# First feed-forward layer: the positive part is written over its PSUM bank, with a new set of planning numbers

## The chip, the cores and the metric

One NeuronCore of a Trainium2 chip runs the whole program. The metric is the time of one execution on the device in microseconds (us). Engines have these names: PE is TensorE (PEld is its weight load), DVE is VectorE, ACT is ScalarE, POOL is GpSimd, SP is the queue that issues the DMAs.

## What is computed

Attention with a hashed mask, then a feed-forward layer with softplus (the layer of the change), then a gated one with SiLU. Shapes: 2 batches, 8 heads, 768 positions, 64 per head; 1536 tokens of 512 for the two layers.

```python
mask = q_bucket[:, :, :, None] == k_bucket[:, :, None, :]
scores = np.where(mask, scale * q @ k.T, -1e9)
attn = exp(scores - max) / (sum + 1e-9)
x = (attn @ v)                       # 1536 x 512
h = x @ w_in                         # 512 -> 2048
g = np.maximum(h, 0.0) + np.log1p(np.exp(-np.abs(h)))
x = g @ w_out                        # 2048 -> 512
gate = x @ w_gate; val = x @ w_val   # 512 -> 1536
out = (gate / (1 + np.exp(-gate)) * val) @ w_out2
```

## The kernel before, in words

Values are split into a high and a low 16-bit part, and a product is three matmuls (L1134 to L1136). The tokens are four chunks of 384, two of each batch. The program has three stages that overlap. Batch 0's attention (scores in fp32, L869, row maximum L888) comes first, while DVE, ACT and POOL unpack the weights of FFN 1. Batch 1's attention (L876, L893) follows, and the matmuls of FFN 1 for chunks 0 and 1 are strewn into it. Then chunks 2 and 3 of FFN 1 run densely on PE while the gate weights are unpacked (L408, L413, L419, L446, L452, L458, L462), and from there FFN 2 (L1262 to L1307) keeps PE to the end.

A tile of FFN 1 is 128 of the 2048 inner features by the 384 tokens of a chunk: 16 tiles a chunk, 64 in all. Its steps, in `ffn1`: 12 matmuls into a PSUM bank `f` (for batch 1, every second tile takes a bank of the ring `z` instead); `mag` on ACT (L1158, |h| into the SBUF tile `fa`); `relu` on DVE (L1163, the positive part into the SBUF tile `fr`); `ex` and `ln` on ACT (L1174, L1177, in place in `fa`); `add` on DVE (L1180, `fr` = `fa` times a scale + `fr`); the high part `g` by ACT, POOL or DVE (L1185, L1188, L1191), the low part on POOL (L1194). Before the change the bank is free once `mag` and `relu` have read it. The ring `f` has two banks, taken in turn; the planes (products with the hash projection, L602 and L607, whose signs DVE takes at L618, or ACT at L627 with POOL at L632), the sums over partitions (L359) and the turned queries (L799) use the same two. Of `fr` and `fa` there are two each.

Nobody writes the order by hand. The class `Order` takes all steps with a length, an engine (or several ways, with a penalty `BV` each) and an urgency (due time plus an offset `U`), and lists them greedily: the step that can start first, but among those of the same engine that could start within `SLACK` of it, the most urgent. Each engine then runs its list strictly in that order. So a different `SLACK`, `BV` or `U` changes the order on every engine and which engine does a step; it doesn't change what is computed.

Of the kernel before, what the change touches and what calls it, by code (L numbers as in the profile page):

```python
# [55 lines left out]
class Order:  # L56
# [5 lines left out]

    LAT = {"EE": 0.0, "AA": 0.15, "GG": 0.1, "VV": 0.13, "EA": 0.2, "EV": 0.2}
    DMA = 1.25, 0.95
    SLACK = 0.1067
    PORT = 0.75

    def __init__(self, rings):
# [120 lines left out]
def tile_hash_attention__softplus_ffn__silu_glu(  # L189
# [39 lines left out]
    def stt(n):  # L229
        return 0.13 + n / 960.0  # L230
# [10 lines left out]
    def pe(cols):  # L241
        return 0.04 + cols / 2400.0

    BV = dict(ck=0.865, re=1.809, st=-2.309, tf=0.612, th=1.227, hi=2.138, lo=5.114, slo=0.082, wlo=0.046, bits=-0.999, meas=1.623, cv=-0.593, ca=0.592)
    U = dict(st=0, vl=0, tp=-20.24, th=-2, tl=-1.85, w2=51.64, qp=-7.63, kp=-4.93, kv=3.56, f1=0.25, y=40, ev=-5.28, ex=2.63, hi=-7.89, lo=2.67, gw=422.36, x=3.11)

    const = ctx.enter_context(tc.tile_pool(name="const", bufs=1))
    xyp = ctx.enter_context(tc.tile_pool(name="xyp", bufs=1))
# [34 lines left out]
    def ways(urgency, opts, after=(), takes=(), uses=(), line=None):  # L283
        return order.step(urgency, opts, after, takes, uses, line)
# [21 lines left out]
    def new(pool, shape, dt, slot):  # L306
        slot.t = pool.tile(shape, dt, tag=slot.ring, name=nm(slot.ring), bufs=RINGS[slot.ring])
        return slot.t
# [829 lines left out]
    def ffn1(c, due, x_ready, w1_ready, g_ready, w2_ready, y_ready):  # L1138

        b = chunks[c][0]  # L1140
        gs, g_done, hs = [], [], []
        for m in range(K1):
            f, fa, fr, g = (Slot(x) for x in ("z" if b == B - 1 and m % 2 else "f", "fa", "fr", "g"))
            gs.append(g)
            gi = m * 128 // G1

            def mm(p, m=m, f=f, g=g):
                if p == 0:
                    bank(f)
                    new(gpool, [128, 2, CN], F16, g)  # L1150
                ps = f.t[:, 0:CN]
                cs = slice(m * 128, (m + 1) * 128)
                for kk in range(p * KD // PARTS, (p + 1) * KD // PARTS):
                    three(ps, w1h[:, kk, cs], w1l[:, kk, cs], xy[c][:, 0, kk], xy[c][:, 1, kk],
                          kk == 0, kk == KD - 1)

            def mag(gi=gi, f=f, fa=fa):
                nc.scalar.activation(  # L1158
                    new(gpool, [128, CN], F32, fa), f.t[:, 0:CN], AF.Abs, scale=sc[b]["inv"][:, gi:gi + 1]
                )  # L1160

            def relu(gi=gi, f=f, fr=fr):
                nc.vector.tensor_scalar(  # L1163
                    new(gpool, [128, CN], F32, fr), f.t[:, 0:CN], sc[b]["invg"][:, gi:gi + 1], 0.0,
                    op0=ALU.mult, op1=ALU.max,
                )

            def relu_a(gi=gi, f=f, fr=fr):
                nc.scalar.activation(
                    new(gpool, [128, CN], F32, fr), f.t[:, 0:CN], AF.Relu, scale=sc[b]["invg"][:, gi:gi + 1]  # L1170
                )

            def ex(fa=fa):
                nc.scalar.activation(fa.t, fa.t, AF.Exp, scale=-1.0)  # L1174

            def ln(fa=fa):
                nc.scalar.activation(fa.t, fa.t, AF.Ln, bias=ones)  # L1177

            def add(fa=fa, fr=fr):
                nc.vector.scalar_tensor_tensor(  # L1180
                    out=fr.t, in0=fa.t, scalar=sc[b]["sg"], in1=fr.t, op0=ALU.mult, op1=ALU.add
                )

            def hi_a(fr=fr, g=g):
                nc.scalar.copy(g.t[:, 0], fr.t)  # L1185

            def hi_v(fr=fr, g=g):
                nc.vector.tensor_copy(g.t[:, 0], fr.t)  # L1188

            def hi_g(fr=fr, g=g):  # L1190
                nc.gpsimd.tensor_scalar(g.t[:, 0], fr.t, 1.0, 1.0, op0=ALU.mult, op1=ALU.mult)  # L1191

            def lo(eng, fr=fr, g=g):
                return lambda: eng.tensor_tensor(g.t[:, 1], fr.t, g.t[:, 0], op=ALU.subtract)  # L1194

            s = None
            for p in range(PARTS):
                s = step(due + 1e3, "E", pe(3 * KD * CN / PARTS) - (0.03 if p else 0.0), lambda p=p, mm=mm: mm(p),
                         x_ready + [w1_ready[gi], s], takes=[] if p else [f, g], uses=[f, g] if p else [], line="f1")
            hs.append(s)  # L1200
            a = step(U["f1"], "A", act(CN), mag, [s, g_ready], takes=[fa], uses=[f])
            r = ways(U["f1"], [("V", stt(CN) + 0.08, relu), ("A", act(CN) + 0.04, relu_a, BV["re"])], [a, g_ready], takes=[fr], uses=[f])
            a = step(U["f1"], "A", act(CN) - 0.04, ex, [a], uses=[fa])
            a = step(U["f1"], "A", act(CN) + 0.04, ln, [a], uses=[fa])
            a = step(U["f1"], "W", stt(CN) + 0.07, add, [a, r], uses=[fa, fr])
            a = ways(U["f1"], [("A", act(CN) - 0.04, hi_a), ("G", gts(CN) + 0.06, hi_g), ("W", dve(CN, 2), hi_v, BV["hi"])], [a], uses=[fr, g])
            a = ways(U["f1"], [("G", gps(CN) + 0.05, lo(nc.gpsimd)), ("W", dve(CN), lo(nc.vector), BV["lo"])], [a], uses=[fr, g])
            g_done.append(a)
        done = []
        nparts = min(YPARTS, K1)  # L1210
        per = K1 // nparts
        for mt in range(KD):
            y = Slot("z" if b == B - 1 else "y")
            s = None
            for p in range(nparts):
                def mm(mt=mt, p=p, y=y):
                    if p == 0:
                        bank(y)
                    cs = slice(mt * 128, (mt + 1) * 128)
                    for kk in range(p * per, (p + 1) * per):  # L1220
                        three(y.t[:, 0:CN], w2h[:, kk, cs], w2l[:, kk, cs], gs[kk].t[:, 0], gs[kk].t[:, 1],
                              kk == 0, kk == K1 - 1)
                s = step(due + 1e3 + U["y"], "E", pe(3 * per * CN), mm,
                         g_done[p * per:(p + 1) * per] + hs + [s] + w2_ready[mt], takes=[] if p else [y],
                         uses=gs[p * per:(p + 1) * per] + ([y] if p else []))

            def hi(mt=mt, y=y):
                nc.scalar.activation(
                    xy[c][:, 0, mt], y.t[:, 0:CN], AF.Copy, scale=sc[b]["yc"][:, mt:mt + 1]
                )  # L1230

            def lo(mt=mt, y=y):
                nc.vector.scalar_tensor_tensor(
                    out=xy[c][:, 1, mt], in0=y.t[:, 0:CN], scalar=sc[b]["yc"][:, mt:mt + 1],
                    in1=xy[c][:, 0, mt], op0=ALU.mult, op1=ALU.subtract,
                )
            a = step(U["f1"], "A", act(CN), hi, [s, y_ready], uses=[y])
            done.append(step(U["f1"], "V", stt(CN), lo, [a], uses=[y]))
        return done
# [228 lines left out]
```

## Time and profile before

| | us |
|---|---|
| median of 3 runs (lowest, highest) | 870.6 (869.28, 871.31) |
| the profiled execution, its own time | 870.66 |
| its span, first to last instruction | 868.9 |
| PE busy in the span | 818.3 |
| DVE busy | 546.1 |
| ACT busy | 441.7 |
| POOL busy | 356.9 |

PE has 94% of the span, but that is an average over stages; the table by stage below says where PE has gaps. A row of the timeline gives start, length, engine, line, operation, output and inputs; "[2.37 <-DVE E L893]" says that the engine stood idle for 2.37 us before this row and that the instruction of line 893 on DVE ended the wait. Matmul rows overlap: each is 0.33 us long, and the next starts 0.16 us later.

### The profile page before, as it was taken

Reading aid. Unit: us, or ns where it says so; the run is one execution under the profiler, and the core shown is the slowest. Engines: PE = TensorE matmul, PEld = TensorE weight load, DVE = VectorE, ACT = ScalarE, POOL = GpSimd, SP = SyncE. Lnnn points to the kernel's source line nnn. Section 1 sums busy time; section 2 is a strip of 40 time slices with the busy share of each in tenths; the row PEclk is TensorE's granted clock in tenths of the full one; section 3 lists DMA queues with packets and bytes.
Section 4 is the critical chain, followed back from the end, with each engine's and each line's share of the span. In section 5 each row is a group of like instructions: output and inputs, shape, how many; then the busy total and the mean of one; then the engine's idle time right before and its main releaser. Section 6 shows DMA issues by size and latency. Waiting matters only on the chain. (4 is left out here: it accounts for less than half of the span.)

```text
span 868.9 us, 14539 instructions
## 1 busy us (share of the span) xinstructions
PE 818.3 (94%) x5576; PEld 530.4 (61%) x5576; DVE 546.1 (63%) x1018; ACT 441.7 (51%) x845; POOL 356.9 (41%) x361
## 2 busy tenths in 40 slices
PE   7999898889989899788999999999999999999998
PEld 3667666545555555455666666555686686677666
DVE  4778896879998678888558789889602301311220
ACT  3445465568788578885778458534302211211220
POOL 0001201669787769986778317413301201210220
PEclk9979999999999999999999999999999999999999
DMA  6224433776859896566683650445000000001001
GB/s 205 71 86 150 149 98 103 170 139 127 199 108 171 160 174 127 113 123 113 126 151 58 206 191 5 143 160 183 1 24 13 2 24 13 1 1 37 1 1 37
DMA packets 179269, 86.10 MB, mean 99 GB/s; under 512 B 141120, under 2 KB 165888, under 8 KB 179200
## 3 DMA queue, kind: packets, MB, share of 16 engines
q1 hardware_dynamic: 179200, 85.17, 41.5%
q8 instruction: 44, 0.72, 0.4%
q14 instruction: 25, 0.20, 0.1%
HBM read 47.35 MB, written 3.15 MB: 58 GB/s over the span
## 5 line engine op out<-in xcount | busy, mean ns | idle before, releaser
L1268 DVE SCALAR_TENSOR_TENSOR sg<-z,smalls,sg 128x384 f32<-128x384 f32 x96 | 59.2, 616 | 176.2 <-ACT sg L1262 174.7
L1277 POOL TENSOR_TENSOR sT<-sg,sT 128x384 fp32r<-128x384 f32 x48 | 51.3, 1069 | 213.5 <-ACT sT L1274 202.1
L929 POOL TENSOR_TENSOR P<-E,P 128x768 f16<-128x768 f32 x72 | 124.5, 1730 | 23.3 <-ACT P L916 19.8
L869 PE MATMUL z<-k,q 128*128 128x384 f32 x192 | 79.5, 543 | 3.3 <-DVE E L888 3.3
L1194 POOL TENSOR_TENSOR g<-fr,g 128x384 f16<-128x384 f32 x64 | 71.3, 1116 | 14.9 <-ACT g L1185 11.3
L1134 PE MATMUL f<-xy,w1h 128*128 128x384 f16 x192 | 62.6, 326 | 4.0 <-DVE fr L1163 1.5
L1134 PE MATMUL z<-xy,wgh 128*128 128x384 f16 x192 | 62.6, 326 | 2.1 <-DVE sg L1268 2.1
L909 ACT ACTIVATE E<-E,st 128x768 f32<-128x768 f32 x48 | 44.7, 931 | 37.3 <-DVE E L888 35.3
L1134 PE MATMUL z<-xy,wvh 128*128 128x384 f16 x192 | 62.6, 326 | 0.0
L1135 PE MATMUL z<-xy,wvh 128*128 128x384 f16 x192 | 62.6, 326 | 0.0
L1136 PE MATMUL z<-xy,wvl 128*128 128x384 f16 x192 | 62.6, 326 | 0.0
L1136 PE MATMUL z<-xy,wgl 128*128 128x384 f16 x192 | 62.6, 326 | 0.0
L1135 PE MATMUL z<-xy,wgh 128*128 128x384 f16 x192 | 62.6, 326 | 0.0
L1136 PE MATMUL f<-xy,w1l 128*128 128x384 f16 x192 | 62.6, 326 | 0.0
L1135 PE MATMUL f<-xy,w1h 128*128 128x384 f16 x192 | 62.6, 326 | 0.0
L1262 ACT ACTIVATE sg<-z,smalls 128x384 f32<-128x384 f32 x48 | 27.8, 580 | 64.2 <-PE z L1136 62.8
L966 PEld LDWEIGHTS <-PT 128*128 128x128 f16 x1296 | 46.5, 99 | 22.0 <-DMA PT<-P 12.2
L1180 DVE SCALAR_TENSOR_TENSOR fr<-fa,smalls,fr 128x384 f32<-128x384 f32 x64 | 54.4, 852 | 5.2 <-ACT fa L1177 2.3
L966 PE MATMUL pv<-v,PT 128*128 128x64 f16 x1296 | 50.2, 194 | 7.8 <-DMA PT<-P 4.9
L1300 PE MATMUL f<-woh,sT 128*128 128x512 f32 x144 | 56.6, 393 | 0.0
L1274 ACT ACTIVATE sT<-sg 128x384 fp32r<-128x384 f32 x48 | 25.0, 522 | 61.0 <-DVE sg L1268 61.0
L1301 PE MATMUL f<-wol,sT 128*128 128x512 f32 x144 | 56.1, 389 | 0.0
(207 smaller groups left out, 2036.6 us busy)
## 6 DMA issues: line engine op xcount, KB each, us to landing
raw64a<-in_moe_w_in_dram SPq DMA_DIRECT2D x16, 512.0 KB, 4.6
raw64a<-in_moe_w_out_dram SPq DMA_DIRECT2D x16, 512.0 KB, 5.0
raw64b<-in_moe_w_gate_dram SPq DMA_DIRECT2D x12, 512.0 KB, 4.4
raw64b<-in_moe_w_val_dram SPq DMA_DIRECT2D x12, 512.0 KB, 4.9
raw64b<-in_moe_w_out_dram SPq DMA_DIRECT2D x12, 512.0 KB, 4.0
rawk<-in_k_dram SPq DMA_DIRECT2D x19, 192.0 KB, 2.9
rawv<-in_v_dram SPq DMA_DIRECT2D x19, 192.0 KB, 3.0
rawq<-in_q_dram SPq DMA_DIRECT2D x16, 192.0 KB, 3.1
```

The lines of the kernel that those rows point to most:

```text
L869: nc.tensor.matmul(a[:, x, 0:HS], lhsT=plain(qd["q"])[:, ts], rhs=plain(kd["k"])[:, x * HS:(x + 1) * HS], start=True, stop=True,)
L929: return lambda: eng.tensor_tensor(P.t[:, 1, :], E.t.rearrange("p a b -> p (a b)"), P.t[:, 0, :], op=ALU.subtract)
L966: nc.tensor.matmul(pv.t[:, t, :], lhsT=PT.t[:, w, kk, :], rhs=values.t[:, kk, c0:c0 + D], start=(kk == 0 and w == 0 and c0 == 0), stop=(kk ...
L1134: nc.tensor.matmul(ps, lhsT=wh, rhs=xh, start=first, stop=False)
L1135: nc.tensor.matmul(ps, lhsT=wh, rhs=xl, start=False, stop=False)
L1136: nc.tensor.matmul(ps, lhsT=wl, rhs=xh, start=False, stop=last)
L1180: nc.vector.scalar_tensor_tensor(out=fr.t, in0=fa.t, scalar=sc[b]["sg"], in1=fr.t, op0=ALU.mult, op1=ALU.add)
L1194: return lambda: eng.tensor_tensor(g.t[:, 1], fr.t, g.t[:, 0], op=ALU.subtract)
L1268: return lambda: nc.vector.scalar_tensor_tensor(out=sg.t, in0=z.t[:, j, 0:CN], scalar=gvs[b, "gv"[j]][:, gi:gi + 1], in1=sg.t, op0=ALU.mul ...
L1277: return lambda: eng.tensor_tensor(sT.t[:, 1, :], sg.t, sT.t[:, 0, :].bitcast(F32), op=ALU.subtract)
L1300: nc.tensor.matmul(ps, lhsT=s[:, 0, cs], rhs=wh, start=(kk == 0), stop=False)
L1301: nc.tensor.matmul(ps, lhsT=s[:, 0, cs], rhs=wl, start=False, stop=False)
```

## The change

`relu` writes the positive part back into the PSUM bank where h stood, instead of into a new `fr`. `add` reads it there, and takes a new `fr` for its result. The bank is now given back after `add`, not after `relu`; `fr` is taken at `add`, not at `relu`. The planner's entry for `add` changes from "W" (DVE, two operands in SBUF, which the planner keeps apart from POOL) to "V" (DVE alone). Beside that `SLACK` and many numbers of `BV` and `U` are new.

```diff
-    SLACK = 0.1067
+    SLACK = 0.1778
-    BV = dict(... st=-2.309, tf=0.612, th=1.227, hi=2.138, lo=5.114, slo=0.082, ... bits=-0.999, ... ca=0.592)
-    U = dict(st=0, vl=0, ... th=-2, ... kp=-4.93, ... y=40, ev=-5.28, ex=2.63, hi=-7.89, lo=2.67, ...)
+    BV = dict(... st=-1.946, tf=0.707, th=1.83, hi=2.138, lo=5.169, slo=0.519, ... bits=-0.311, ... ca=-0.057)
+    U = dict(st=1.92, vl=2.04, ... th=5.65, ... kp=0.64, ... y=32.5, ev=-3.23, ex=11.42, hi=-14.89, lo=1.89, ...)
             def relu(gi=gi, f=f):
                 nc.vector.tensor_scalar(
-                    new(gpool, [128, CN], F32, fr), f.t[:, 0:CN], sc[b]["invg"][:, gi:gi + 1], 0.0,
+                    f.t[:, 0:CN], f.t[:, 0:CN], sc[b]["invg"][:, gi:gi + 1], 0.0,
                     op0=ALU.mult, op1=ALU.max,
                 )
-            def add(fa=fa, fr=fr):
+            def add(f=f, fa=fa, fr=fr):
                 nc.vector.scalar_tensor_tensor(
-                    out=fr.t, in0=fa.t, scalar=sc[b]["sg"], in1=fr.t, op0=ALU.mult, op1=ALU.add
+                    out=new(gpool, [128, CN], F32, fr), in0=fa.t, scalar=sc[b]["sg"], in1=f.t[:, 0:CN], op0=ALU.mult, op1=ALU.add
                 )
-            r = ways(... [a, g_ready], takes=[fr], uses=[f])
+            r = ways(... [a, g_ready], uses=[f])
-            a = step(U["f1"], "W", stt(CN) + 0.07, add, [a, r], uses=[fa, fr])
+            a = step(U["f1"], "V", stt(CN) + 0.08, add, [a, r], takes=[fr], uses=[f, fa])
```

The order moves on every engine. Three places matter below.

ACT, in chunk 1 of FFN 1 (`fa` belongs to FFN 1, `E` and `st` to the attention of batch 1), before:

```order
L1158 ACTIVATE fa_742_3756<-f_736_3726,smalls_87 128x384
L909 ACTIVATE E_740_3742,sum_738_3740<-E_740_3742,st_739_3741,smalls_87 128x768
L1174 ACTIVATE fa_742_3756<-fa_742_3756 128x384
L904 ACTIVATE st_746_3775<-st_746_3775,smalls_87 128x1
L1158 ACTIVATE fa_752_3809<-f_744_3761,smalls_87 128x384
L1177 ACTIVATE fa_742_3756<-fa_742_3756,smalls_87 128x384
```

The same engine and chunk in the changed kernel:

```order
L1174 ACTIVATE fa_767_3826<-fa_767_3826 128x384
L1177 ACTIVATE fa_767_3826<-fa_767_3826,smalls_87 128x384
L1158 ACTIVATE fa_771_3837<-f_765_3812,smalls_87 128x384
L1174 ACTIVATE fa_771_3837<-fa_771_3837 128x384
L1177 ACTIVATE fa_771_3837<-fa_771_3837,smalls_87 128x384
L904 ACTIVATE st_769_3834<-st_769_3834,smalls_87 128x1
```

The three ACT steps of a tile stood apart, with work of the attention between; now they stand together.

DVE, after the chain of small operations that works out batch 1's scales (L1085 to L1125), before:

```order
L1115 TENSOR_SCALAR smalls_87<-smalls_87 128x1
L1121 TENSOR_SCALAR smalls_87<-smalls_87 64x4 x2
L1125 TENSOR_SCALAR smalls_87<-smalls_87 128x1
L893 TENSOR_SCALAR E_911_4762,st_910_4761<-z_897_4629 128x768
L1233 SCALAR_TENSOR_TENSOR xy1_132<-y_891_4583,smalls_87,xy1_132 128x384
```

The same chain's end in the changed kernel:

```order
L1121 TENSOR_SCALAR smalls_87<-smalls_87 64x4 x2
L1125 TENSOR_SCALAR smalls_87<-smalls_87 128x1
L1163 TENSOR_SCALAR f_844_4233<-f_844_4233,smalls_87 128x384
L1033 TENSOR_TENSOR xn_659_3195<-pv_833_4163,sum_788_3944 128x3x64
L1028 RECIPROCAL sum_817_4082<-sum_817_4082 128x3
L1180 SCALAR_TENSOR_TENSOR fr_854_4329<-fa_849_4313,smalls_87,f_844_4233 128x384
```

Behind the chain stood a row maximum and the write-out of a bank `y` of the layer's output; now a tile of FFN 1 with its bank stands there.

DVE at the start of FFN 2 (L1420 are its scales, L1268 frees a bank of `z`, `w32b` is the unpacking of the last weights), before:

```order
L1420 TENSOR_SCALAR smalls_87<-smalls_87 128x6 x4
L408 TENSOR_SCALAR w32b_1191_6928<-raw64b_1189_6922 128x1024
L413 SCALAR_TENSOR_TENSOR w32b_1191_6928<-raw64b_1189_6922,w32b_1191_6928 128x1024
L419 SCALAR_TENSOR_TENSOR w32b_1191_6928<-raw64b_1189_6922,w32b_1191_6928 128x1024
L408 TENSOR_SCALAR w32b_1194_6959<-raw64b_1190_6925 128x1024
L1268 SCALAR_TENSOR_TENSOR sg_1193_6957<-z_1188_6897,smalls_87,sg_1193_6957 128x384
L413 SCALAR_TENSOR_TENSOR w32b_1194_6959<-raw64b_1190_6925,w32b_1194_6959 128x1024
L1268 SCALAR_TENSOR_TENSOR sg_1193_6957<-z_1188_6897,smalls_87,sg_1193_6957 128x384
```

The same place in the changed kernel:

```order
L1420 TENSOR_SCALAR smalls_87<-smalls_87 128x6 x4
L1268 SCALAR_TENSOR_TENSOR sg_1214_6999<-z_1210_6943,smalls_87,sg_1214_6999 128x384 x2
L408 TENSOR_SCALAR w32b_1215_7003<-raw64b_1211_6968 128x1024
L413 SCALAR_TENSOR_TENSOR w32b_1215_7003<-raw64b_1211_6968,w32b_1215_7003 128x1024
L1268 SCALAR_TENSOR_TENSOR sg_1218_7034<-z_1213_6974,smalls_87,sg_1218_7034 128x384 x2
```

Both L1268 of the first tile moved ahead of the unpacking.

Between the two lists of all engines, these counts of instructions differ most: signs of the planes on DVE (L618) 69 to 47, on ACT (L627) 1 to 23 with as many offsets on POOL (L632); the high part of `g` on ACT 34 to 20, on POOL 30 to 44. The 9120 entries of PE are the same in kind and number, in another order.

## Rows read from the trace of the kernel before

**Rows 1.** Stages: window, length, busy PE, PEld, DVE, ACT, POOL, clock, DMA share, GB/s.
```profile
20.48:165.00 144.52, 132.22 (x710) 91.03 (x709) 113.17 (x230) 73.47 (x131) 22.56 (x27) 0.95 0.39 115
245.00:421.00 176.00, 156.11 (x1515) 96.98 (x1514) 143.79 (x295) 133.12 (x282) 138.67 (x144) 0.98 0.75 138
512.00:548.00 36.00, 34.95 (x219) 21.19 (x217) 33.17 (x48) 31.57 (x60) 22.39 (x23) 1.00 0.19 60
587.30:868.90 281.60, 277.78 (x1536) 188.66 (x1535) 78.48 (x113) 63.97 (x112) 51.31 (x48) 1.00 0.07 25
```
**Rows 2.** Waits of PE and DVE: who for whom, total us, times, longest.
```profile
PE z L876 <- DVE E L893: 5.6, 5, 2.4
PE z L869 <- DVE E L888: 3.3, 6, 1.6
PE pv L966 <- DVE fr L1180: 2.8, 1, 2.8
PE y L1134 <- DVE xy L1233: 3.7, 1, 3.7
PE f L1134 <- DVE fr L1163: 1.5, 2, 0.9
PE f L607 <- DVE fr L1163: 1.3, 2, 0.7
PE z L1134 <- DVE fr L1163: 1.1, 1, 1.1
DVE E L893 <- POOL P L929: 11.3, 9, 2.8
```
**Rows 3.** Single lines: duration of one in ns, least/median/most; first and last start.
```profile
L1180 DVE SCALAR_TENSOR_TENSOR fr<-fa,smalls,fr x64: 603/619/2014, 178.1 to 550.5; 128x384 f32<-128x384 f32 x64
L1268 DVE SCALAR_TENSOR_TENSOR sg<-z,smalls,sg x96: 604/618/621, 585.0 to 842.0; 128x384 f32<-128x384 f32 x96
L618 DVE TENSOR_SCALAR k<-f,smalls x37: 656/685/689, 12.3 to 412.1; 64x384 f32<-64x384 f32 x22, 64x384 f16<-64x384 f32 x15
L632 POOL TENSOR_SCALAR k<-hb,smalls x1: 650/650/650, 320.9 to 320.9; 64x384 f16<-64x384 f16 x1
```
**Rows 4.** Groups by form: busy us, mean ns of one, idle before it.
```profile
L1180 DVE SCALAR_TENSOR_TENSOR fr<-fa,smalls,fr 128x384 f32<-128x384 f32 x64 | 54.4, 852 | 5.2 <-ACT fa L1177 2.3
L1177 ACT ACTIVATE fa<-fa,smalls 128x384 f32<-128x384 f32 x64 | 38.9, 610 | 0.6
L1174 ACT ACTIVATE fa<-fa 128x384 f32<-128x384 f32 x64 | 32.9, 516 | 0.5
L1158 ACT ACTIVATE fa<-f,smalls 128x384 f32<-128x384 f32 x48 | 27.7, 577 | 18.1 <-PE f L1136 12.9 <-DVE fr L1180 3.0 <-PE f L607 1.3
```
**Rows 5.** Timeline of POOL and DVE near 201 us.
```profile
200.53 1.65 POOL L929 TENSOR_TENSOR P<-E,P 128x768 f16<-128x768 f32 x1
200.60 0.62 DVE L1163 TENSOR_SCALAR fr<-f,smalls 128x384 f32<-128x384 f32 x1
201.14 1.46 DVE L1180 SCALAR_TENSOR_TENSOR fr<-fa,smalls,fr 128x384 f32<-128x384 f32 x1
```
**Rows 6.** Timeline near 359 us: DVE, and PE behind it.
```profile
356.93 1.26 DVE L1180 SCALAR_TENSOR_TENSOR fr<-fa,smalls,fr 128x384 f32<-128x384 f32 x1
358.91 1.20 DVE L1180 SCALAR_TENSOR_TENSOR fr<-fa,smalls,fr 128x384 f32<-128x384 f32 x1
360.62 0.94 DVE L893 TENSOR_SCALAR_CACHE_REDUCE E<-z 128x768 f32<-128x768 f32 x1
361.63 1.25 PE L876 MATMUL z<-k,q 128*128 128x384 f16 x4 [2.37 <-DVE E L893]
```
**Rows 7.** Timeline: batch 1's scale chain on DVE, its first and last row.
```profile
396.19 0.16 DVE L371 TENSOR_SCALAR f<-f 128x3 int32<-128x3 int32 x1
403.23 0.15 DVE L1125 TENSOR_SCALAR smalls<-smalls 128x1 f32<-128x1 f32 x1
```
**Rows 8.** Timeline of PE: the start of FFN 2.
```profile
587.32 0.32 PE L1134 MATMUL z<-xy,wgh 128*128 128x384 f16 x1 [2.12 <-DVE sg L1268]
```

## What the change was predicted to do, before it ran

> **What bounds the kernel now.** I read the table of stages first, then the waits of PE, then the places in the timeline behind the longest of them. In FFN 2, from 587.3 us on, PE is busy 277.78 of 281.60 us [rows 1]: nothing that happens on another engine can shorten that. The time to be won lies ahead of it, in what PE does not do there: 12.3 us of 144.52 in the first attention stage and 19.9 us of 176.00 in the second, both length minus busy [rows 1]. In the second stage DVE is busy 143.79, POOL 138.67 and ACT 133.12 us of 176 [rows 1]. These engines work through lists in a fixed order, so at 75 to 82% they already make PE wait now and then. The waits name DVE most often: 5.6 us for the row maximum of batch 1 (L893), 3.3 for that of batch 0, 2.8 behind an `add`, 3.7 for the write-out of `y`, and 1.5 + 1.3 + 1.1 us for banks that `relu` still holds [rows 2]. So the question is whether the change takes work off DVE faster than it adds waits for banks.
>
> The sum is made against the profiled execution, 870.66 us (span 868.9 and 1.8 around it). The median of the runs shown is 870.6, so the two can be taken as one. A difference under 0.2% (1.7 us) I call no change, as that is about what a measurement of this kernel can tell.
>
> **The add on DVE.** `add` reads two tiles in SBUF. Its median is 619 ns but its mean is 852, and the longest took 2014 [rows 3, 4]. Rows 5 show why: the `add` that starts at 201.14 ends at 202.60, after the POOL instruction that started at 200.53 ended at 202.18; it lasted 1.46 us. The `relu` at 200.60, which reads one operand, in PSUM, ran 0.62 us under the same POOL instruction [rows 5]. The multiplication of FFN 2 (L1268) has the operands that the new `add` will have, one tile in PSUM and one in SBUF, and in 96 instances never took more than 621 ns [rows 3]. So I cost the new `add` at 618 ns: (852 - 619) x 64 = 14.9 us of DVE time go. Of these some 10.6 us lie in chunks 0 and 1 (17 of the 27 stretched ones, among them the three in rows 5 and 6), where the attention waits for DVE.
>
> How much of the 14.9 us reaches PE? At 361.63 PE had waited 2.37 us for a row maximum that stood behind two adds of 1.26 and 1.20 us; at 619 each, 1.2 us of the 2.37 would have gone, half [rows 6]. The DVE-ended waits that are of this kind are 5.6 + 3.3 + 2.8 = 11.7 us [rows 2]. Half of them would be 5.9, but not each has a stretched add in front. The ends are 0 (DVE's gain falls into its own idle time) and 10.6 + 5.5 = 16 us (all of it, with the signs below, reaches PE). I take 5, near the half that rows 6 show.
>
> By the Trainium skill, Perfetto Trace Analysis, Optimizing Scalar/DVE Operations, an access costs DVE about 60 ns in SBUF and about 125 in PSUM, which speaks against this change. It would make the `add`, and the `relu` that now also writes to PSUM, some 65 ns longer each, an estimate from that page of 64 x 0.13 = 8.3 us of DVE time, and leave 6.6 of the 14.9; the term of 5 us below would be 2.2, and the time 868.6. For the reading the trace disagrees: 618 ns with a PSUM operand, 619 without [rows 3]. For a wide write into PSUM no run here shows it.
>
> From the rows alone, a `relu` that writes into PSUM is bounded by 0 and 0.07 us more than now: the plane signs (L618), the same kind of instruction on as many columns, take 685 ns where the `relu` takes 0.62 us [rows 3, 5]. That is 0 to 4.5 us of DVE time. I take 0, since no operand in PSUM shows in the durations of L1268.
>
> **The signs.** 22 of 69 signs leave DVE (685 ns each [rows 3]): 14 in the first attention stage, 9.6 us of its 113.17 us DVE time [rows 1], and 8 in the second, 5.5 us. PE's waits for DVE in the first stage are small (part of the 3.3 us). Ends 0 and 3.3; I take 1. The price is on POOL: about 12 of the new offsets at 650 ns [rows 3] fall in the stage where POOL has 138.67 of 176 us, 7.8 us more, and DVE already waits 11.3 us there for POOL's low part (L929) to give back a buffer `E` [rows 1, 2]. Ends 0 (in POOL's idle time) and 7.8; since it is a fifth idle, I take a fifth, 1.5 us lost.
>
> **The banks.** From the last matmul of a tile, the old bank is held for `mag` and `relu`, at least 0.58 + 0.62 us. The new one is held for `mag`, `ex`, `ln` and `add`: 0.58 + 0.52 + 0.61 + 0.62 = 2.3 us [rows 3, 4]. That is the least; a row maximum (0.94 us) stands between `relu` and `add` in 12 of the first 32 tiles, and each step is handed on between engines. I take 3.3 us, with ends 2.6 and 4.0. Against this the new order on PE gives room: I counted the PE work between a tile's last matmul and the next use of the same bank. By the spacing of their starts in the trace, a tile of 12 matmuls counts 1.95 us, a `pv` of 18 short ones 0.73, a score of batch 1 0.65, a pair of plane products 0.33. In chunks 0 and 1 the room is 1.7 to 6.8 us. Seven of 32 tiles have less than 2.6 us; in the old order there were nine. The order on ACT helps as well: the three steps of a tile now stand together, where a 1 us exponential and a small operation used to stand between.
>
> The sum of what is missing (hold minus room, where positive) is 4.1 us at a hold of 2.6, 10.0 at 3.3 and 20.2 at 4.0. Behind the waiting matmul stand the scores and `pv` of the attention, since PE goes strictly in order; behind these the row maxima. But a wait for a bank takes the place of other waits, since whatever PE needed next gets ready in the meantime. I let half of 10.0 through, 5.0 us. The old bank waits of 1.5 + 1.3 us go [rows 2]. Net: 2.2 us lost; ends -0.8 (half of 4.1) and 17.4 (all of 20.2).
>
> **The scale chain.** On DVE the chain of batch 1's scales takes from 396.19 to 403.38, 7.2 us [rows 7]. Behind it stood the write-out of `y`, and PE waited 3.7 us [rows 2]. In the new order a `relu`, two small operations and an `add` stand there, so a bank comes free about 7.2 + 0.62 + 0.5 + 0.62 = 8.9 us after the chain's product, and PE has 1.95 + 0.73 + 1.95 = 4.6 us of work until it needs that bank. The old wait goes, a new one of 4.3 us comes: 0.6 lost.
>
> **The dense part and FFN 2's start.** In 512 to 548 us tiles of chunk 3 follow each other every 1.95 us; with the high part often on ACT it was busy 31.57 of 36, fell behind, and the bank came late: 1.1 us [rows 1, 2]. Now `mag`, `ex` and `ln` are 1.70 us a tile, below 1.95, the high part is mostly on POOL, and four banks leave 5.9 us of room: the 1.1 us go, although the hold is longer. What covers it is POOL, 22.39 of 36 us busy [rows 1]; without it the hold would grow tile by tile as before. At the start of FFN 2 PE waited 2.12 us for L1268, which stood behind unpacking [rows 8]; both L1268 of the first tile now stand ahead of it, ready 2 us before PE needs the bank: 2.1 go. Nothing is late next there, since PE then has its own work to the end.
>
> **Sum.** -5 (adds) - 1 (signs) + 1.5 (POOL) + 2.2 (banks) + 0.6 (chain) - 1.1 - 2.1 = -4.9 us: 870.66 - 4.9 = 865.8 us.
>
> **Rivals.** First, slower: the bank decides. If the hold is about 3.7 us and what is missing (15 us) is paid in full, the term is +12.2 and not +2.2, and the time 875.8 us. It turns from a gain to a loss where the bank term passes 7.1 us, that is at a hold of 3.3 if all of the missing room is paid, at 4.0 if half is. For it speaks that DVE and ACT are busy enough to delay each of four steps; against it that the old order had as many tight places. The Trainium skill, Perfetto Trace Analysis, Optimization Strategy, says that recurring gaps can come from too little PSUM for the next tile, which is this rival's mechanism; the traces so far show it in small waits only [rows 2].
>
> Second, no change: the freed DVE time falls into DVE's idle time. Without the -5 and the -1 the sum is +1.1, 871.8 us. For it speaks that POOL and ACT are nearly as busy as DVE in that stage [rows 1].
>
> Third, a large gain: DVE's relief comes through at 10 us, the bank term is at its low end and POOL costs nothing: 870.66 - 10 - 1 - 0.8 + 0.6 - 3.2 = 856.3 us. Against it speaks that other engines end waits too.
>
> Fourth, it may not do what it says: most rows of the order moved because of the new numbers, not because of the bank. Then the clock may move too. In the first attention stage the mean granted clock is 0.95 [rows 1]: some 14 of the 144.5 us were at 1.2 GHz and the rest at 2.4, which cost up to 7 us. If half of that goes, or as much again comes, with the changed order, the time moves by 3.6 us either way. That widens each case and favours none.
>
> **How the numbers follow.** The forecast of 865.8 us (860 to 869) has 0.48, the slower rival 0.25 (870 to 881), no change 0.16, the large gain 0.11. The range of 8 in 10 goes from 855 to 877: it takes in no change, the middle of the slower rival and most of the large gain. Faster by over 0.2% is the forecast and the large gain, 0.58 after a small part of the forecast that falls within 0.2%; within 0.2% is 0.16; slower 0.26.
>
> **What would show it.** Right: no `add` over 0.65 us; DVE's busy time down by some 30 us; the waits of PE for L893 at half; no wait at FFN 2's first tiles; bank waits named `add` (L1180) of some 5 to 9 us with the chain's. Wrong: bank waits of 15 us and more, a hold over 4 us in chunk 1, longer waits of DVE for POOL, or a `relu` well above 0.62 us.

## The result, and the profile after

| | before | after |
|---|---|---|
| median of 20 runs each, us | 871.21 | 880.06 |
| lowest and highest, us | 866.0, 882.17 | 870.62, 885.72 |
| the profiled execution, its own time and span, us | 870.66, 868.9 | 883.05, 881.3 |
| mean granted clock of the profiled execution | .985 | .977 |

The changed kernel is slower: the ratio is 1.0071, with an interval of 1.0043 to 1.0099. It is estimated from the single runs, without the slowest of each kernel, and comes to 6.2 us (3.7 to 8.6), where the medians lie 8.9 us apart. Forecast were 865.8 us in a range of 855 to 877; the median lies 3 us above its upper end. Over its 20 runs, time and granted clock go together: the eight runs at a clock of .978 or more took 870.6 to 874.4 us, the twelve at less 876.3 to 885.7.

First the stages of the changed kernel, in windows cut as in [rows 1], with the last two moved by the 12 to 15 us that the program is late there. The second row, 40 to 60 us, is new; behind the table stands the same stretch of the kernel before. Columns: window, length, busy PE, PEld, DVE, ACT, POOL, clock, DMA share, GB/s.

```profile
20.48:165.00 144.52, 131.97 (x687) 92.57 (x687) 105.83 (x216) 79.86 (x139) 31.68 (x32) 0.91 0.37 110
40.00:60.00 20.00, 19.23 (x64) 13.10 (x64) 8.39 (x18) 8.06 (x15) 2.45 (x3) 0.53 0.39 132
245.00:421.00 176.00, 152.30 (x1470) 91.94 (x1468) 128.76 (x281) 139.14 (x284) 141.15 (x157) 0.97 0.75 136
527.00:563.00 36.00, 35.02 (x217) 21.18 (x216) 29.74 (x45) 32.26 (x56) 23.68 (x30) 1.00 0.27 90
599.70:881.30 281.60, 277.69 (x1538) 188.69 (x1535) 85.25 (x118) 64.76 (x113) 52.74 (x48) 1.00 0.08 27
```
```profile
40.00:60.00 20.00, 18.15 (x76) 11.40 (x74) 12.47 (x27) 8.79 (x15) 0.19 (x1) 0.74 0.32 104
```

DVE has what was promised: 105.83 instead of 113.17 us in the first stage and 128.76 instead of 143.79 in the second [rows 1]. PE has gained nothing from it: it does 23 matmul records fewer in the first stage and 45 fewer in the second, in the same length. In the first stage that isn't idle time. PE is busy as long as before, and the granted clock is .91 instead of .95; between 40 and 60 us it is .53.

Then single lines as in [rows 3], the relu (L1163) among them: duration in ns, least, median, most.

```profile
L1180 DVE SCALAR_TENSOR_TENSOR fr<-fa,smalls,f x48: 586/613/616, 181.0 to 560.2; 128x384 f32<-128x384 f32 x48
L1180 DVE SCALAR_TENSOR_TENSOR fr<-fa,smalls,z x16: 597/615/616, 469.1 to 562.2; 128x384 f32<-128x384 f32 x16
L1163 DVE TENSOR_SCALAR f<-f,smalls x48: 605/625/627, 179.6 to 558.9; 128x384 f32<-128x384 f32 x48
```

The relu of the kernel before, which wrote into SBUF:

```profile
L1163 DVE TENSOR_SCALAR fr<-f,smalls x48: 603/615/619, 172.8 to 547.5; 128x384 f32<-128x384 f32 x48
```

No add is stretched any more; the longest took 616 ns, where it was 2014 [rows 3]. The relu that writes into PSUM takes 625 ns at the median, where it took 615 into SBUF.

The waits, as in [rows 2], with the wait of `pv` for the transposed probabilities (`PT`), which was 4.9 us in 5 waits before:

```profile
PE pv L966 <- DMA PT<-P: 15.0, 17, 2.9
PE f L1134 <- DVE fr L1180: 6.1, 3, 5.0
PE z L943 <- ACT E L909: 5.5, 3, 4.3
PE z L876 <- DVE E L893: 4.8, 4, 2.7
DVE E L893 <- POOL P L929: 19.1, 14, 2.8
```

The held bank is small among them: 6.1 us, and 5.0 of these are one wait, behind the chain of scales. On DVE that chain lies between two rows as in [rows 7], a relu and an add follow, and PE waits behind these:

```profile
369.96 0.17 DVE L371 TENSOR_SCALAR f<-f 128x3 int32<-128x3 int32 x1
...
378.07 0.15 DVE L1125 TENSOR_SCALAR smalls<-smalls 128x1 f32<-128x1 f32 x1
378.14 0.62 DVE L1163 TENSOR_SCALAR f<-f,smalls 128x384 f32<-128x384 f32 x1
379.01 0.59 DVE L1180 SCALAR_TENSOR_TENSOR fr<-fa,smalls,f 128x384 f32<-128x384 f32 x1
```
```profile
379.65 0.48 PE L1134 MATMUL f<-xy,w1h 128*128 128x384 f16 x1 [4.96 <-DVE fr L1180]
```

Last the place where the clock falls, the timeline of PE from 37.9 us on. The matmul that sums a weight's squares over the partitions (L359) waits 1.36 us for ACT, whose unpacking (L446) stands behind a cast that waited for a scale; a second gap of 0.77 us follows. First PE, then ACT.

```profile
37.94 0.49 PE L799 MATMUL f<-ident,rawq 128*64 128x128 f32 x3
39.78 0.38 PE L359 MATMUL f<-smalls 128*128 128x1 f32 x2 [1.36 <-ACT w1h L446]
40.94 1.27 PE L774 MATMUL z<-ident,rawk 128*64 128x128 f32 x6 [0.77 <-DVE E L888]
42.13 1.64 PE L602 MATMUL f<-q,pjf 64*128 64x384 f32 x2
...
52.63 5.38 PE L982 MATMUL pv<-rawv,PT 128*128 128x64 f32 x24
57.81 4.73 PE L869 MATMUL z<-k,q 128*128 128x384 f32 x8
```
```profile
37.51 1.15 ACT L452 ACTIVATE w1h<-w32a,smalls 128x1024 f16<-128x1024 f32 x1 [3.69 <-DVE smalls L377]
38.58 1.06 ACT L446 ACTIVATE w1h<-w32a 128x1024 f16<-128x1024 f32 x1
```

A product of two planes (L602, x2) takes 1.64 us here and 0.91 at full clock. The low level, 1.2 GHz, lasts until 62 us. The Trainium skill, TensorE: Matmul & The Clock Gate, HAM oscillation, tells of such a pattern with longer waits, for DMAs, in every round of a loop: they throw the clock back, and the work behind pays at half rate. The rows agree that the clock is low behind the waits and that the work takes nearly twice as long; that waits as short as 1.36 and 0.77 us came before it, only the rows show.

So the question for the experiments was which of these makes the lost time: the held bank, the chain of scales, the low clock, or the order that the new numbers make.

### The profile page after: what moved, and what is told of

Read it like the earlier page. It is cut to its first block, busy times and chain, and to the rows that moved or that the text cites. A ratio compares the mean times of both kernels' runs of the same rounds, so it can differ in the third digit from the quotient of the medians.

```text
span 881.3 us, 14539 instructions
## 1 busy us (share of the span) xinstructions
PE 823.9 (93%) x5576; PEld 533.1 (60%) x5576; DVE 513.1 (58%) x990; ACT 465.2 (53%) x859; POOL 378.1 (43%) x398
## 4 chain that ended last, share of the span: by engine, by line
PE 59%; DMA 15%; DVE 10%; POOL 8%; ACT 3%; issue 3%; SPq 1%; POOLq 0%; ACTq 0%; DVEq 0%
PE z L1134 10%; PE z L1136 10%; PE z L1135 10%; DMA PT<-P 9%; POOL P L929 4%; PE f L1302 4%; PE f L1300 4%; PE f L1301 4%; PE z L869 3%; PE f L602 2%; PE f L1134 2%; DMA raw64a<-in_moe_w_out_dram 2%; PE f L1135 2%; PE f L1136 2%; PE pv L982 2%
## 5 line engine op out<-in xcount | busy, mean ns | idle before, releaser
L1268 DVE SCALAR_TENSOR_TENSOR sg<-z,smalls,sg 128x384 f32<-128x384 f32 x96 | 59.2, 617 | 172.9 <-ACT sg L1262 171.1
L929 POOL TENSOR_TENSOR P<-E,P 128x768 f16<-128x768 f32 x72 | 121.9, 1695 | 30.5 <-ACT P L916 27.7
L869 PE MATMUL z<-k,q 128*128 128x384 f32 x192 | 76.5, 528 | 3.1 <-DVE E L888 2.1
L1134 PE MATMUL f<-xy,w1h 128*128 128x384 f16 x192 | 64.3, 335 | 9.5 <-DVE fr L1180 6.1
L1194 POOL TENSOR_TENSOR g<-fr,g 128x384 f16<-128x384 f32 x64 | 64.5, 1009 | 7.5 <-ACT g L1185 3.7
L1135 PE MATMUL f<-xy,w1h 128*128 128x384 f16 x192 | 64.2, 334 | 0.0
L888 DVE TENSOR_SCALAR_CACHE_REDUCE E<-z 128x768 f32<-128x768 f32 x48 | 45.6, 951 | 21.2 <-PE z L869 14.7
L893 DVE TENSOR_SCALAR_CACHE_REDUCE E<-z 128x768 f32<-128x768 f32 x48 | 45.6, 951 | 19.3 <-POOL P L929 19.1
```

Of the source, the lines that this page charges most:

```text
L869: nc.tensor.matmul(a[:, x, 0:HS], lhsT=plain(qd["q"])[:, ts], rhs=plain(kd["k"])[:, x * HS:(x + 1) * HS], start=True, stop=True,)
L888: nc.vector.tensor_scalar(new(att, [128, 2, HS], F32, E), z.t[:, :, 0:HS], PLAIN_TOP, None, op0=ALU.min, op1=ALU.min, accum_out=a[:, 1:2],)
L893: nc.vector.tensor_scalar(new(att, [128, 2, HS], F32, E), z.t[:, :, 0:HS], MASK_FLOOR, None, op0=ALU.max, op1=ALU.max, accum_out=a[:, 0:1],)
L929: return lambda: eng.tensor_tensor(P.t[:, 1, :], E.t.rearrange("p a b -> p (a b)"), P.t[:, 0, :], op=ALU.subtract)
L1134: nc.tensor.matmul(ps, lhsT=wh, rhs=xh, start=first, stop=False)
L1135: nc.tensor.matmul(ps, lhsT=wh, rhs=xl, start=False, stop=False)
```

## The experiments

Times are medians of 6 or 12 runs. Each kernel shared its chip with runs of the kernel before, whose median there stood between 869.55 and 871.47 us; "+8.9" is the distance to that. The ratio in brackets, with its 95% interval, is estimated from the single runs; it doesn't follow the medians exactly and can differ from the distance by 3 us. A time of this kind is uncertain by some 3 us, and up to 5 where there are 6 runs, as the intervals show, so that a difference of 2 us decides nothing.

### The change and its numbers apart: e1 and e2

e1 is the changed code with the old `SLACK`, `BV` and `U`; e2 the old code with the new ones.

```diff
 # e1, against the changed kernel
-    SLACK = 0.1778
+    SLACK = 0.1067
 (and the old lines BV and U)
```

> The changed kernel with SLACK, BV and U of the kernel before: the positive part goes over its bank, the planning numbers are the old ones, no sign goes to ACT and POOL (0 of 70). Theory A (the new numbers cost: signs on ACT and POOL and a later low part make the transposed P late, PE's waits for DMA grew from 4.9 to 15.0 us): 864 to 871 us, waits of PE for the transposed P near 5 us. Theory B (the bank held until the sum costs): 876 to 882 us, waits of PE named L1180 of 6 us or more. Theory C (the start, where the clock stays longer at the lower level): as before, 871 us, if the mean granted clock is 0.985 again.

> The kernel before with the new SLACK, BV and U; the positive part stays in SBUF and the bank is free after it. 19 of 70 signs on ACT. Theory A: 876 to 882 us, waits of PE for the transposed P of 10 us or more. Theory B: 869 to 872 us. Theory C: 876 to 882 us with a mean granted clock near 0.976, the waits of the second attention stage as before.

e1 took 910.31 us, +40.8 (ratio 1.0463, 1.0416 to 1.0509); e2 881.43, +11.9 (1.0142, 1.0099 to 1.0184). None of the three theories had e1 so slow. In e1 the waits for the bank are again small, 7.5 us. The loss stands elsewhere in the trace: the `mag` of tile 17 of FFN 1, the first of chunk 1, begins at 399.9 us, where it began at 326.1 before, and between 245 and 320 us PE works 53 of 75 us, at a low clock besides:

```profile
245.00:320.00 75.00, 53.03 (x509) 30.12 (x505) 58.53 (x123) 55.65 (x123) 59.73 (x64) 0.86 0.90 166
```

So the change is dear in the plan, not as waits for the bank. A reading that fits, and that e8 below tests, is that with the old numbers the planner finds a free bank too seldom to fill the attention's gaps with tiles. The planner's entry for `add` (V for W) and the later taking of `fr` are part of e1 too, and no run takes these apart from the bank. The new numbers remedy the loss, and cost something of their own.

The long early low clock of the changed kernel comes with the new numbers and not with the change: between 40 and 60 us the granted clock is 1.00 in e1, and in e2, whose code is the old one, it is .51:

```profile
40.00:60.00 20.00, 20.00 (x62) 13.34 (x60) 7.80 (x17) 7.02 (x13) 2.46 (x3) 0.51 0.32 108
```

### The operand and the signs: e3 and e4

e3 keeps the changed kernel's order instruction by instruction, but the positive part goes into the space of `g` in SBUF, so that the bank is free behind the relu and the add reads two SBUF tiles. e4 puts the plane signs back on DVE.

```diff
 # e3: g's 2 x 384 fp16 seen as 384 fp32
+            def positive(g):
+                return g.t.rearrange("p w n -> p (w n)").bitcast(F32)
-                    f.t[:, 0:CN], f.t[:, 0:CN], sc[b]["invg"][:, gi:gi + 1], 0.0,
+                    positive(g), f.t[:, 0:CN], sc[b]["invg"][:, gi:gi + 1], 0.0,
 (the same in relu_a; add reads positive(g))
 # e4
-    BV = dict(... bits=-0.311, ...)
+    BV = dict(... bits=-0.999, ...)
```

> The changed kernel, every engine's order the same, but the positive part goes into the space of g in SBUF (which is not written until later), and the bank is free after it, as before the change; the sum then reads two operands in SBUF. Theory A: 878 to 884 us, since the order is the same, and the sums are stretched again (mean 0.8 us for 0.62). Theory B: 868 to 874 us, PE's waits named L1180 gone. Theory C: 878 to 884 us, clock near 0.976.

> The changed kernel with one planning number set back (bits -0.999 for -0.311), so that 66 of 70 signs are on DVE again, 4 on ACT and POOL. Theory A in its narrow form (POOL's share of the signs delays the low part): 868 to 874 us, waits of PE for the transposed P at 8 us or less. Theory B: 878 to 882 us. Theory C: 871 to 875 us only if the mean granted clock rises to 0.984.

e3 took 890.26 us, +20.7 (1.0213, 1.0168 to 1.0258): with the bank free early it is some 12 us slower than the changed kernel, and slower than any of the theories had it. Its adds are stretched again, as their line shows (least, median, most), and the wait behind the chain of scales is there although the bank is free after the relu. The second row, of PE's waits, is the same in e3 and in e12 below, which has the same order:

```profile
L1183 DVE SCALAR_TENSOR_TENSOR fr<-fa,smalls,g x64: 589/656/2092, 179.1 to 572.5; 128x384 f32<-128x384 f32 x64
```
```profile
PE f L1134 <- DVE g L1166: 4.6, 1, 4.6
```

e4 took 887.54 us, +18.0 (1.0192, 1.0155 to 1.0229), with 12.2 us of waits for L893 and 17.8 for the transposed probabilities, although its clock between 40 and 60 us is 1.00. That, too, is slower than any theory had it. As the planner moves other steps along with the signs, e4 doesn't show what the signs alone are worth. But POOL's 23 offsets don't explain the longer waits for the probabilities: in e4 only 4 are left, in e1 none, and the waits are there (17.8 and 15.5 us).

### The early low clock and more banks: e5 to e8

e5 is the changed kernel once more. e6 adds ten matmuls of the identity with itself in the two early gaps, into the bank `y`, which nobody uses until much later. e7 gives FFN 1's tiles in batch 0 that bank as a third one; e8 is the same with the old numbers.

```diff
 # e6: 6 ahead of the 34th step on PE, 4 ahead of the 35th
+    y0 = Slot("y"); new(ps_y, [128, 512], F32, y0)
+    order.filler = {("E", n): lambda k=k: [nc.tensor.matmul(y0.t[:, 0:128], lhsT=ident, rhs=ident,
+        start=True, stop=True) for _ in range(k)] for n, k in ((34, 6), (35, 4))}
 # e7, e8
-            ... Slot(x) for x in ("z" if b == B - 1 and m % 2 else "f", "fa", "fr", "g"))
+            ... Slot(x) for x in ("z" if b == B - 1 and m % 2 else "y" if b < B - 1 and m % 3 == 2 else "f", "fa", "fr", "g"))
```

> The changed kernel as it is, as the yardstick of the next three on the same chip. Expected as in its first runs: about 880 us at a granted clock of .975, single runs near 871 at a clock of .98 and above; granted clock of the stretch 40 to 60 us about .53 in runs near 880.

> The changed kernel, and ten matmuls of the identity with itself into the y bank, which nobody uses yet, in the two gaps of 1.36 and 0.78 us at 38.4 and 40.2 us, behind which the granted clock falls to .50 until 62 us. If that early low clock is where the lost time comes from: the clock of 40 to 60 us stays near 1.00, and the kernel takes 5 to 9 us less, 871 to 875. If the attention is held by its waits for the transposed probabilities and not by the clock: the clock of that stretch rises, the waits grow by what it gives, and the time stays at 878 to 881.

> The changed kernel, but in batch 0 every third tile of FFN 1 takes the bank of ring y, which is idle until FFN 1's second matmul, so that tiles go through three banks and the longer hold is paid for. The planner then places the last tile of chunk 1 before 756 of the 1296 matmuls onto pv, where the changed kernel has it before 972. If the held bank is what costs, by the tiles that come too late: 865 to 872. If the early clock or the attention's own chain costs: 878 to 884, and waits for the transposed probabilities stay at 15 us or more.

> The code of the change with the numbers of before, and the third bank for every third tile of batch 0. Without the third bank this took 910 us, its tiles lagging far behind the attention (tile 17 began at 400 us). If banks are what its tiles lacked: tile 17 begins before 350 us and the time falls by 20 us or more, to 875 to 890. If the order of urgencies makes them lag whatever the banks: 900 to 912.

e5 took 880.27 us (+8.9; 1.0078, 1.0039 to 1.0116), e6 873.51 (+2.2; 1.0034, 1.0003 to 1.0064). Ten matmuls of no use take 6.8 us off the kernel by the medians, 3.8 by the ratios. Below, e6's timeline with the fillers (L351), and its stretch of 40 to 60 us:

```profile
35.20 1.50 PE L351 MATMUL y<-ident 128*128 128x128 f32 x12
37.35 0.38 PE L359 MATMUL f<-smalls 128*128 128x1 f32 x2 [0.64 <-ACT w1h L446]
37.59 1.14 PE L351 MATMUL y<-ident 128*128 128x128 f32 x8
38.57 0.82 PE L774 MATMUL z<-ident,rawk 128*64 128x128 f32 x6
39.32 0.91 PE L602 MATMUL f<-q,pjf 64*128 64x384 f32 x2
```
```profile
40.00:60.00 20.00, 19.47 (x117) 14.20 (x117) 14.74 (x26) 12.33 (x22) 8.16 (x6) 1.00 0.39 121
```

PE gets through 117 records there instead of 64. The time is won as the first theory said, and the 12 runs now lie at clocks of .976 to .992, where those of e5 lay at .965 to .987. The quick runs of the changed kernel, at clocks of .978 and more, take as long as those of e6; whether the early low clock was missing in them, no trace shows, since only slower ones were kept.

e7 took 885.24 us (+13.9; 1.0167, 1.0113 to 1.0221), so its theory falls: banks are not what the changed kernel lacks. The tiles do come earlier, but then they are used up, and the attention is left alone with its own waits. Between 320 and 400 us PE is fuller than in any of the others (before: 70.55 us), and between 400 and 480 it is empty for 17 us:

```profile
320.00:400.00 80.00, 78.13 (x721) 48.54 (x719) 56.86 (x136) 66.22 (x139) 69.44 (x82) 1.00 0.61 114
400.00:480.00 80.00, 63.23 (x655) 39.78 (x654) 38.35 (x82) 56.13 (x105) 52.33 (x50) 0.87 0.73 131
```

e8 took 895.32 us (+24.0; 1.0269, 1.0221 to 1.0317) against the +40.8 of e1, with the `mag` of tile 17 at 361.4 us instead of 399.9. That is 17 us back, less than the 20 asked for, and the tile later than the 350 us. With the old numbers the supply of banks is thus a good part of the loss, and not all of it.

### The chain of scales, with the gap filled: e9 to e12

e9 is the kernel before with its own early gap filled (8 matmuls, 42 us). That gap is 1.56 us long, and the mean clock of .74 between 40 and 60 us means some 10 us at 1.2 GHz; they lie from 44 to 55 us (the expectation says 53):

```profile
43.67 2.15 PE L982 MATMUL pv<-rawv,PT 128*128 128x64 f32 x12 [1.56 <-DVE PT L974]
```

In e10 the small instructions of batch 1's scales (25; the expectation says 27) are no longer issued in a row; one or two go ahead of each following step on DVE, and the early gap is filled as in e6. e11 is the kernel before with the same two edits, e12 is e3 with the gap filled.

```diff
 # e10, e11: x_scale, g_scales, y_scales become generators, with a yield behind each instruction
-        gr = step(0, "V", 0.8, lambda b=b: g_scales(b), ...)
+        gr = step(0, "V", 0.8, lambda b=b: order.later.append(g_scales(b)) if b else list(g_scales(b)), ...)
 # in Order, ahead of every step
+        any(next(x, 0) for x in self.later if eng in "VW")
```

> The kernel before, with eight matmuls of the identity in its one early gap ahead of a low clock (1.56 us at 42.1 us, low from 44 to 53 us). If its times between 865 and 876 are spread by that same clock: clock of 40 to 60 us 1.00 instead of .74, and about 4 us less, 866 to 869; the change is then worth 5 to 7 us more time at equal early clocks (873.5 with the gap filled). If the fillers delay the chain behind them: 871 to 874, and the change costs next to nothing once the clock is held.

> The changed kernel with the early gap filled, as in e6 (873.5 us), and batch 1's chain of scales (27 small instructions in a row on DVE, 7.2 us) handed out one instruction ahead of each following DVE step. If the bank that waits behind that chain costs what the wait shows: the wait of FFN 1's tile of 4.8 us goes, with the low clock behind it, and the kernel takes 4 to 7 us less, 867 to 870. If the attention's chain is late there anyway: the wait turns into waits for the transposed probabilities and second passes, 872 to 875.

> The kernel before with the early gap filled and the same chain of scales handed out. In the kernel before no bank waits behind the chain; its longest wait there is 3.7 us of FFN 1's second matmul. If that wait costs what it shows: 3 us under the kernel with the gap alone filled; otherwise the same as that. Beside e10 it shows what the change is worth with both side effects taken away.

> The changed kernel's order with the positive part in SBUF and the bank free behind it, as in e3 (890.3 us at clock .966), and the early gap filled. If the 10 us between e3 and the changed kernel were the clock: 874 to 878, so that the operand in PSUM is worth little. If they are DVE's longer sums (847 against 608 ns on 64 of them, 15 us of DVE time): 882 to 886, still about 10 us above e6.

e9 took 872.87 us (+1.4; 1.0017, .9983 to 1.0051): in the kernel before, the filled gap wins nothing, although the clock of 40 to 60 us rises to 1.00. e10 took 870.42 (-1.1; 1.0009, .9981 to 1.0037), e11 867.82 (-3.7; .9977, .9945 to 1.0008). In e10 the wait behind the chain is gone (the longest behind L1180 is 1.6 us, in e6 4.8), but PE is no fuller for it between 320 and 400 us: 63.69 us busy, in e6 63.84. With both edits the changed kernel and the kernel before stand 2.6 us apart, which these runs can't tell from nothing.

e12 took 879.47 us (+8.0; 1.0126, 1.0082 to 1.017). It has e6's order and e6's fillers, and lacks only the sum in PSUM: 5.8 us more by the medians, 8.0 by the ratios, between the two forecasts. So the operand in PSUM is worth 6 to 8 us in a fixed order, even after it has paid for the held bank.

### What is left: e13 to e16

e13 is e2, so the new numbers without the change, with gap and chain treated as in e10 and e11. e14 is e10 with 14 more fillers in a gap of 3.7 us at 113 us. e15 and e16 are the chain handed out, without fillers, in the kernel before and in the changed one.

> The code of before with the new numbers (e2: 881.4 us), the early gap filled and the chain of scales handed out. The kernel before treated so takes 867.8 us, the changed one 870.4. If the new numbers cost only by the early low clock: 867 to 870, and the change itself (operand in PSUM, bank held) is worth nothing or a little more time. If the new order costs by itself and the operand gives some of it back: 873 to 878.

> The changed kernel with the early gap filled and the scales handed out (e10: 870.4 us), and 14 more matmuls of the identity in the gap of 3.7 us ahead of a transpose of E at 113 us, behind which the profiled run of e10 had the low clock from 118 to 135 us. If that gap costs by the clock in most runs: 866 to 868, below the kernel before. If it does so in few, or if the fillers hold up the attention: 869 to 873.

> The kernel before with the chain of scales handed out and no fillers. With both it took 867.8 us, with the fillers alone 872.9. If the chain of scales alone makes the difference: 866 to 869. If the fillers are needed for it, or the 867.8 was chance: 870 to 872.

> The changed kernel (880.3 us) with the chain of scales handed out and no fillers. If chain and early clock are independent costs: about 3 us less, 877, still with the low clock at 40 to 60 us. If the chain's wait matters only once the clock is held: 879 to 881.

e13 took 874.27 us (+3.4; 1.0027, .9998 to 1.0055), 7.1 more than e11 by the medians and 4.4 by the ratios, which is just beyond their uncertainty: the new numbers cost by their order itself, beyond the early clock. In the trace it looks like e7's pattern, PE full early and short of work later. First e13, then e11, 320 to 400 and 400 to 480 us:

```profile
320.00:400.00 80.00, 77.25 (x724) 48.38 (x723) 60.67 (x128) 67.03 (x138) 70.08 (x73) 1.00 0.62 117
400.00:480.00 80.00, 66.79 (x623) 40.59 (x622) 52.71 (x103) 57.99 (x108) 52.24 (x50) 0.85 0.68 117
```
```profile
320.00:400.00 80.00, 69.79 (x674) 43.82 (x672) 61.64 (x123) 64.87 (x139) 68.06 (x72) 0.94 0.67 115
400.00:480.00 80.00, 78.17 (x729) 49.35 (x726) 54.62 (x110) 59.53 (x114) 57.28 (x58) 1.00 0.70 116
```

The changed kernel has its hole elsewhere, so this pattern is not what its own order costs. PE is short of work between 320 and 400 us, where it does 594 records (before: 692), and full behind that. First the changed kernel, then the one before:

```profile
320.00:400.00 80.00, 61.88 (x594) 36.47 (x593) 61.58 (x141) 60.81 (x123) 63.08 (x70) 0.94 0.68 127
400.00:480.00 80.00, 76.73 (x743) 48.40 (x742) 39.20 (x77) 57.75 (x109) 54.05 (x55) 1.00 0.64 110
```
```profile
320.00:400.00 80.00, 70.55 (x692) 44.46 (x691) 65.99 (x133) 67.26 (x141) 69.90 (x74) 0.98 0.64 124
```

In that stretch it waits 7.2 us for the transposed probabilities (before: 0.5), 5.1 for banks behind `add` and 4.5 for the row maximum. The hole is there in e6 and e10 too, with 618 and 628 records. What in the new order makes it was not tested.

e10, which differs from e13 by the change itself (and by what the planner makes of it), is 4.5 us faster than e13 by the medians and 1.6 by the ratios, which can't be told from nothing.

e14 took 871.78 us (+0.9; 1.0009, .998 to 1.0037): nothing won beside e10, so the second gap is no cause in the median. e16 took 879.19 (+8.9; 1.0079, 1.004 to 1.0117), the same as e5: the chain alone wins nothing measurable there, and with the early clock held 3.2 us (e6 to e10), no more than the uncertainty. e15 took 866.70 (-3.6; .9946, .9913 to .998). It is the one kernel here that is measurably faster than the one before, and it beats the changed one by 12 us.

## Why the prediction was wrong

The table puts neighbours side by side. Each number is the difference of their distances to the kernel before on the same chip, once by the medians and once by the ratios, and uncertain by 3 to 5 us. The second and the fourth can't be told from nothing.

| from, to | what differs | us, medians | us, ratios |
|---|---|---|---|
| e5 to e6 | early gap filled, clock held | -6.8 | -3.8 |
| e6 to e10 | chain of scales handed out | -3.2 | -2.2 |
| e11 to e13 | the new numbers' order, both treated | +7.1 | +4.4 |
| e13 to e10 | the change itself, both treated | -4.5 | -1.6 |
| e6 to e12 | sum in SBUF, same order | +5.8 | +8.0 |

**The step that failed** is the fourth rival. It said that most rows moved because of the new numbers and that the clock might move with them, priced this at 3.6 us either way "and favours none". It got no chance of its own and no sign, so the sum of -4.9 us holds nothing for it. The runs show a loss of 8 to 14 us in its place: 4 to 7 by the clock behind one place, and 4 to 7 by the order. These prices hold on this road alone: without the change the new numbers cost 11.9 us (e2), and without the new numbers the change costs 40.8 (e1). What in the order costs, beyond the clock, stays open. The clock's part could have been looked for, since order and trace were there: in the new order on ACT a cast that waits for a scale stands ahead of the unpacking that PE's sum needs, at a place where PE had little else. Its price was bounded too low as well. Its 3.6 us came from the stage's mean of .95 [rows 1], which went to .91: over 144.5 us that is 5.8 us of work at full clock. Of these, 3.2 lie between 40 and 60 us, where 19.23 busy us at .53 did the work of 10.2 at full clock, and before 18.15 at .74 did that of 13.4.

Most of what was named as a sign of being right came true: no add over 0.65 us, DVE's busy time down by 33 us, no wait at FFN 2's first tiles, 6.1 us of bank waits. The time went the other way all the same, because the loss lies in what the sum left out.

The band of 1.7 us that the prediction called no change was too narrow: the 20 runs of the kernel before spread over 16 us.

**Adds, -5.** The relief came in full on DVE (546.1 to 513.1 us busy, signs included, and no add over 616 ns). In a fixed order it was worth 6 to 8 us, net of the bank (e6, e12), no less than its size. But PE's waits for L893, which were to halve, only went from 5.6 [rows 2] to 4.8 us: in the new order the gain doesn't show where the prediction looked for it.

**Signs, -1, and POOL, +1.5.** e4, with the signs back on DVE, is 9 us slower than the changed kernel, at a better early clock, but the planner moved all else too, so neither sign nor size of the first term can be read from it. The POOL term was worked out the wrong way round: POOL was busy 138.67 of 176 us [rows 1], so a fifth of the 7.8 us would fall into its idle time and four fifths, 6.2, would be lost. DVE waits 19.1 us for POOL's L929 instead of 11.3 [rows 2], and PE's waits for the probabilities grew from 4.9 to 15.0. But e1, with no offset on POOL, has 16.8 us of DVE's waits, and all orders but the old one have 12 to 20 us of PE's, with or without offsets, so they belong to the order.

**Banks, +2.2.** As waits the held bank costs 1.1 us beside the chain's, so the term was too large, and the slower rival (the bank decides, 875.8) came near the time by luck, on another road than its own. What no step considered is that the change also works on the plan: e1 shows 40.8 us with the old numbers, of which a third bank gives 17 back (e8). The new numbers buy that back, and cost the 8 to 14 us above. Whether other numbers would buy it back more cheaply stays open.

**Scale chain, +0.6.** The new wait was forecast at 4.3 us and is 4.96; the old one of 3.7 [rows 2] shrank to 1.7. It held. What I hadn't seen is that the chain as a whole is worth 3.6 us in the kernel before (e15).

**Dense part -1.1, FFN 2's start -2.1.** From the first `mag` of chunk 2 to the end the changed kernel is 4.3 us faster, where these terms gave 3.2: that `mag` begins 16.7 us later (465.42 against 448.75), and the profiled span is 12.4 us longer. Both waits are gone, so both terms held.

**The write into PSUM.** The relu took 625 ns into PSUM against 615 into SBUF, both at the median, so the term of 0 for it was nearly right. The 65 ns more for each access, an estimate from Perfetto Trace Analysis, Optimizing Scalar/DVE Operations, in the Trainium skill, do not show for the write either.

## What to carry to other kernels

Where a planner lays out the order, predict the planner's numbers as a change of their own: run the change with the old numbers and the new numbers without it before you believe either. Look in the new order for early places at which PE will wait; what such a place costs need not be the gap of 2 us, it can be the 20 us at half clock behind it. A handful of idle matmuls there bought time back once (e6) and nothing twice (e9, e14), so measure it. And filler work may have a best time: e1 lost time with its tiles late, and e7 and e13 look like orders with their tiles too early, which was not tested further.

## What the chip showed that I had not expected

Behind two gaps of 1.36 and 0.77 us lay 20 us at 1.2 GHz, and ten matmuls took 4 to 7 us off an 880 us kernel. In the kernel before, a gap of 1.56 us with the low clock from 44 to 55 us behind it gave nothing when it was filled (e9). Why the one pays and the other does not was not tested; that other engines set the pace there before is a guess.

An add with two SBUF operands took up to 2092 ns beside POOL's work (e3), where the same add with one of them in PSUM never took more than 617 in any run. By SBUF — State Buffer, Who interferes with whom, in the Trainium skill, a DVE instruction with two inputs in SBUF contends with one of GpSimd that reads SBUF, and one with at most one such input, outside the two-port modes, doesn't; the rows agree.
